# Gated delta-rule attention and softplus MLP on one core: head pairs over two batches, single inverses for chunks 0 and 1, a new order of work

## The chip, the core and the metric

The kernel runs on one core of a Trainium2 chip. TensorE (PE; its weight loads are listed apart as PEld) multiplies matrices into PSUM, VectorE (DVE), ScalarE (ACT) and GpSimd (POOL) do the rest, and SyncE (SP), ACT and POOL issue the transfers. Each engine takes its own instructions in their order and waits on semaphores for the others. The metric is device time in microseconds (us), the median of several runs; lower is better.

## What is computed

Each of 32 sequences (4 batches x 8 heads) of 768 tokens with 48 features keeps a 48x48 state. The output of all heads goes, token by token, through a two-layer MLP.

```python
k_n = k / (norm(k) + 1e-6)
for t in range(768):                        # per batch b and head h
    y[t]  = g[t] * (q[t] @ state)
    v_old = k_n[t] @ state
    state = state + beta[t] * outer(k_n[t], v[t] - v_old)
x   = y as [3072 tokens, 384]               # 8 heads x 48
out = softplus(x @ w_in) @ w_out            # 384 -> 2048 -> 384
```

## The kernel before

**Tiling.** The 768 tokens are 12 chunks of 64. In a chunk the recurrence becomes matrix products: the gram matrix of the keys, the inverse of a triangular 64x64 matrix for each sequence, and products with the state. The 32 sequences lie as 2 partition halves (`r`, batches 2r and 2r+1) times 16 units. Small matmuls have 64 rows by 64 columns of the array, so four tiles: row half by column half.

**Stages of a chunk.** `norms` (L341): squares, a row reduction (`red`), root, `eps`. `front` (L388): `cast` or `kmul` scales and casts k and q, `trs` transposes them on PE, `kev`/`qev` evict to `kqt`, `gram` (L516) multiplies, `kkc` and `mask` (L498) evict. `inverse` (L567) works for a group of chunks: `ln` transposes 32x32 blocks so that each lane has its own small matrix, `prep` scales it, 15 `step`s of a multiply (L664) and an add (L671) invert the 16x16 diagonal blocks on DVE or POOL, `ca`, `cb` and three `st` transposes (L714) bring them back, and `xmm`, `tmm`, `zmm` on PE join the blocks. `chain` (L811) is the recurrence from chunk to chunk: `ks` and `qs` (L826) multiply keys and queries with the state, `w`, `umm` (L880), `zu` (L893), `smm` (L910) with the state's update `s`, `ymm` (L936) for the output product, `y` (times g), `ytr` (transposes) and `xt`. `dense` (L976) is the MLP: `g1` (L989) into bank `h`, `soft` (L1001, softplus on ACT), `g2` (L1016) into bank `o`, `o` (eviction), `store`. Jobs are one chunk for chunks 0, 1, 10 and 11, and two chunks between.

**Groups.** `GROUPS` joins two chunks to one inverse, so that the lanes hold both; chunks 0 and 1 are group 0. For that group (`DIAGONALS`) `gramd` (L540) multiplies the 32x32 diagonal blocks apart, 64 matmuls a chunk, so that `ln` needs them alone. Chunks 0 and 1 are `RAW`: their keys are used without norm, and `lbeta` (L580 to L583) puts the norms into beta.

**Pairs.** Two heads of one batch (`2i`, `2i+1`, the index `m`) share a transposed tile; `p` is the batch in a half. The loops that use the units in turn walk

```python
CROSS = [(r, p, i, m) for i in range(NP) for m in range(2) for p in range(2) for r in range(2)]
```

`umm` and `zu` read half `r` and write half `r ^ p`. `ymm` reads rows `HALF[r]` and writes columns `HALF[r]`, bank `yp[m]`.

**Order.** Nothing is scheduled while it runs. Every piece of work is an item with a number, and `_ORDER` (L1066) lists them in one sequence, each with its engine's letter (P, D, A, G for POOL, S for SP). An engine's queue is its items in this sequence; buffers are handed out and returned in it too. `fill` items (L1046) are four matmuls of the identity into bank `h` whose result isn't used; 40 exist, 13 stand in the order, two of them behind the first `g1`. Loads are issued by SP: two of 192 KB for each of k, q, v and g a chunk, in 192-byte rows but for q (1,536 bytes). The weights are issued by POOL, w_in and w_out in four parts each, between its other work.

Of the kernel before, what the change touches and what calls it, by code (L numbers as in the profile page):

```python
# [11 lines left out]
F16 = mybir.dt.float16  # L12
# [68 lines left out]
GROUPS = [[0, 1], [2, 3], [4, 5], [6, 7], [8, 9], [10, 11]]  # L81
GROUP_OF = [i for i, cs in enumerate(GROUPS) for _ in cs]
INV_ENG = ["DG"] * 6
N_FILL = 40
DIAGONALS = (0,)

@with_exitstack
def kernel(
# [11 lines left out]
    nc = tc.nc  # L100
# [39 lines left out]
    r_kn = ring("kn", 4, [P, 2, H, 64], F16)  # L140
# [35 lines left out]
    make_identity(nc, ident32)  # L176
    for r in range(2):
        for x in range(2):
            l0 = 32 * (2 * r + x)
            bt = beta[2 * r : 2 * r + 2].rearrange("p h (c l) -> c (p h) l", l=C)  # L180
            nc.gpsimd.dma_start(
                out=beta_l[l0 : l0 + 32, 0], in_=bt[:2, :, HC * x : HC * x + HC]
            )
# [23 lines left out]
    def copy(en, o, x, sign=1):  # L207
# [9 lines left out]
        [(r_kk, 0, 1), (r_td, 0, 1), (r_z, 1, 0), (r_z, 1, 1)],  # L217
        [(r_, n, a) for r_ in (r_kk, r_td) for n in (1, 2) for a in range(2)]
# [23 lines left out]
    for n in range(1, 4):  # L242
# [7 lines left out]
        for i in FIXED[n] if n < 3 else []:  # L250
# [3 lines left out]
            if i[0] is r_z or i[2] == 0 or n == 1:  # L254
                i[0].init.setdefault(i[1], []).append(setup[n][-1])
    beta_it = []
    for r in range(2):
        for x in range(2):
            for a in range(2):

                def bload(en, r=r, x=x, a=a):
# [3 lines left out]
                        out=beta_l[l0 : l0 + 16, 1:],  # L265
# [12 lines left out]
    def heads(ap, m):  # L278
        return ap.rearrange("p a (i m) d -> p (a i) m d", m=2)[:, :, m]
# [11 lines left out]
    def load(name, x, r, c, b2):  # L291
# [5 lines left out]
        def fn(en):  # L297
            if name == "q":
                src = x[:, b2::2, t0 : t0 + C].rearrange(
                    "b i (g j) d -> b i g (j d)", j=8  # L300
                )
                ENG[en].dma_start(out=b.ap[:, b2].rearrange("p h d -> p (h d)"), in_=src)
                return
            o = b.ap[64 * b2 : 64 * b2 + 64]
# [5 lines left out]
        its.append(add("load", f"{name}{c}.{b2}", "S", fn, bufs=[b], size=192))  # L310

    for c in range(NC):
        for name, x, r in (("k", k, r_f), ("q", q, r_f), ("v", v, r_f), ("g", g, r_f)):
            for b2 in range(2):
                load(name, x, r, c, b2)
# [19 lines left out]
    kd_of, kd_it = {}, {}  # L335
# [5 lines left out]
    def norms(c):  # L341
        kf, kl = tiles["k", c]
        ksq = Buf(r_f)
        if RAW[c] and c % 2:
            nv = nv_of[c - 1]
        else:
            nv = Buf(r_nv)
# [7 lines left out]
        n0 = NU * (c % 2) if RAW[c] else 0  # L355

        def nvs():
            return nv.ap[:, n0 : n0 + NU]
# [804 lines left out]
```

## Time and profile before

| | |
|---|---|
| runs | 242.04, 242.27, 242.74 us, median 242.27 |
| profiled execution | span 241.5 us from first to last instruction (its own time isn't listed; the runs' median is 0.77 above the span) |
| dense matmuls on PE | L1016 77.7 us, L989 74.0 us |
| fills (L1046) on PE | 18.1 us |
| softplus (L1001) on ACT | 56.5 us |
| DMA | 27.57 MB, 114 GB/s mean |
| chain that ended last | PE 75%, DMA 7%, DVE 6%, SP's queue 4%, issue 3%, ACT 2%, POOL 1% |

The page's slices (40 of 6 us, tenths of busy time, the last lines the granted TensorE clock and the DMA engines):

```
PE   7645877879988999999999999999999999999983
DVE  2768699888897889987899757896496310623000
ACT  5767576764982778876895767757363674143540
POOL 8740393875779778989597482016620000000000
PEclk9985599999999999999999999999999999999999
DMA  6999989999999399961889514962302311303112
```

In a group of the profile, "x384 | 8.5, 187 | 0.4 <-DVE u" means 384 instructions, 8.5 us of busy time together (overlaps count once), 187 ns for one, and 0.4 us in which the engine was idle just before them, with what ended the wait. A line can be that of a helper: L209, L211 and L213 are `copy`, told apart by their tiles. "SPq" is SP's queue of transfers.

### The profile page before, as it was taken

To read this page: it belongs to the slowest core of one execution; us is meant where nothing else is said; L and a number is where in the kernel's file an instruction comes from. 1 tells how busy PE (TensorE), PEld (TensorE's weight loads), DVE (VectorE), ACT (ScalarE), POOL (GpSimd) and SP (SyncE) were. 2 spreads that over 40 slices of the span, in tenths; PEclk is the share of its full clock that TensorE was granted. 3 is DMA by queue.
4 is the path that set the end of the run, shared out by engine and by line. 5 is a ranking of instruction groups with operands and counts; after the bars stand their busy time and mean duration, and the time that the engine had idled before them with its cause. 6 is when DMAs were issued, how large, how long until landed. Compare 5 with 4: busy or idle time off the path is not lost.

```text
span 241.5 us, 11396 instructions
## 1 busy us (share of the span) xinstructions
PE 219.4 (91%) x5020; PEld 135.6 (56%) x5020; DVE 161.7 (67%) x368; ACT 152.8 (63%) x292; POOL 113.7 (47%) x197
## 2 busy tenths in 40 slices
PE   7645877879988999999999999999999999999983
PEld 2423455646764664556655566655565555677751
DVE  2768699888897889987899757896496310623000
ACT  5767576764982778876895767757363674143540
POOL 8740393875779778989597482016620000000000
PEclk9985599999999999999999999999999999999999
DMA  6999989999999399961889514962302311303112
GB/s 102 182 245 137 167 135 190 176 173 180 180 217 167 57 177 164 162 113 35 150 153 184 97 30 94 160 122 52 69 21 52 68 34 25 64 19 81 35 33 65
DMA packets 86833, 27.57 MB, mean 114 GB/s; under 512 B 77048, under 2 KB 86776, under 8 KB 86784
## 3 DMA queue, kind: packets, MB, share of 16 engines
q1 hardware_dynamic: 80624, 20.83, 52.6%
q0 software_dynamic: 3840, 3.17, 8.5%
q10 hardware_dynamic: 2320, 2.85, 5.2%
q8 instruction: 39, 0.64, 1.2%
q14 instruction: 10, 0.08, 0.1%
HBM read 25.26 MB, written 4.72 MB: 124 GB/s over the span
## 4 chain that ended last, share of the span: by engine, by line
PE 75%; DMA 7%; DVE 6%; SPq 4%; issue 3%; ACT 2%; POOL 1%; DVEq 0%; ACTq 0%; POOLq 0%
PE o L1016 27%; PE h L989 26%; DMA w_in<-in_moe_w_in_dram 4%; PE d L826 3%; SPq L305 3%; PE d L936 3%; PE d L516 2%; DMA f<-in_q_dram 2%; PE d L422 2%; PE d L963 2%; PE d L454 2%; PE d L880 2%; PE d L910 2%; PE d L893 2%; PE d L768 1%
## 5 line engine op out<-in xcount | busy, mean ns | idle before, releaser
L1016 PE MATMUL o<-w_out,ga 128*128 128x384 f16 x384 | 77.7, 327 | 0.7 <-ACT osb L209 0.6
L1001 ACT ACTIVATE ga<-h 128x512 f16<-128x512 f32 x96 | 56.5, 599 | 29.8 <-PE h L989 25.9
L989 PE MATMUL h<-xt,w_in 128*128 128x512 f16 (+1 forms) x384 | 74.0, 327 | 0.5 <-DMA w_in<-in_moe_w_in_dram 0.3
L989 PEld LDWEIGHTS <-w_in 128*128 128x128 f16 x384 | 34.5, 98 | 21.2 <-DMA w_in<-in_moe_w_in_dram 0.8
L1016 PEld LDWEIGHTS <-ga 128*128 128x128 f16 x384 | 33.7, 98 | 21.8 <-issue 0.8
L664 POOL TENSOR_TENSOR tmp<-nn,tt 128x78 f32<-128x78 f32 (+7 forms) x53 | 19.2, 362 | 16.1 <-DVE tt L671 13.0
L373 POOL TENSOR_TENSOR nv<-nv,half_c 128x16 f32<-128x16 f32 x8 | 23.5, 2940 | 6.6 <-DVE nv L362 6.5
L671 POOL TENSOR_TENSOR tt<-tt,tmp 128x78 f32<-128x78 f32 (+7 forms) x53 | 20.4, 385 | 4.2
L498 DVE TENSOR_TENSOR mt<-d,mask 128x256 f16<-128x256 f32 x48 | 18.2, 413 | 4.5 <-PE d L516 3.5
L209 ACT ACTIVATE kqt<-d 128x1024 f16<-128x1024 f16 (+1 forms) x18 | 18.0, 1000 | 4.8 <-PE d L454 3.6
L211 DVE CAST u<-d 128x384 f16<-128x384 f32 x20 | 10.9, 554 | 14.3 <-PE d L880 7.9
L209 ACT ACTIVATE u<-d 128x384 f16<-128x384 f32 x28 | 13.0, 490 | 11.8 <-PE d L880 5.4
L1046 PE MATMUL h<-ident 128*128 128x512 f16 x52 | 18.1, 493 | 1.7 <-DVE ident L197 1.7
L209 ACT ACTIVATE kk<-d 128x256 f16<-128x256 f32 x37 | 13.4, 386 | 6.3 <-PE d L516 5.4
L209 ACT ACTIVATE osb<-o 128x384 f32<-128x384 f32 x19 | 9.3, 492 | 9.4 <-PE o L1016 9.3
L454 PE MATMUL d<-ident,qn 128*128 128x128 f16 x96 | 8.5, 243 | 6.7 <-ACT qn L209 5.9
L950 DVE TENSOR_TENSOR yg<-d,f 128x384 f16<-128x384 f32 x24 | 12.3, 551 | 2.9 <-PE d L936 2.8
L924 DVE TENSOR_TENSOR s<-s,d 128x384 f16<-128x384 f16 x20 | 10.4, 542 | 5.7 <-PE d L910 4.3
L644 POOL TENSOR_TENSOR nn<-ln,beta_l 128x256 f32<-128x256 f16 x8 | 6.1, 780 | 14.2 <-DVE ln L627 14.2
L209 ACT ACTIVATE xt<-d 128x768 f16<-128x768 f16 x10 | 8.1, 813 | 7.0 <-PE d L963 7.0
L866 DVE TENSOR_TENSOR w<-f,d 128x384 f16<-128x384 f32 x22 | 11.3, 545 | 1.4 <-ACT xt L209 0.7
L362 DVE TENSOR_REDUCE nv<-f 128x16 f32<-128x768 f32 x12 | 11.3, 942 | 1.0 <-ACT f L351 1.0
(117 smaller groups left out, 346.7 us busy)
## 6 DMA issues: line engine op xcount, KB each, us to landing
f<-in_k_dram SPq DMA_DIRECT2D x24, 192.0 KB, 5.7
f<-in_q_dram SPq DMA_DIRECT2D x24, 192.0 KB, 5.6
f<-in_v_dram SPq DMA_DIRECT2D x24, 192.0 KB, 5.3
f<-in_g_dram SPq DMA_DIRECT2D x24, 192.0 KB, 5.3
out_dram<-osb ACTq DMA_DIRECT2D x29, 96.0 KB, 2.7
out_dram<-osb SPq DMA_DIRECT2D x19, 96.0 KB, 2.8
w_in<-in_moe_w_in_dram POOLq DMA_DIRECT2D x4, 384.0 KB, 7.9
w_out<-in_moe_w_out_dram POOLq DMA_DIRECT2D x4, 384.0 KB, 8.4
```

The costliest lines, as they stand in the source:

```text
L209: nc.scalar.activation(o, x, AF.Copy, scale=float(sign))
L362: lambda en: nc.vector.tensor_reduce(nvs().rearrange("p (a h) -> p a h", a=2), ksq.ap, mybir.AxisListType.X, ALU.add),
L373: nc.gpsimd.tensor_tensor(nvs(), nvs(), half_c[:, :NU], ALU.pow)
L454: nc.tensor.transpose(o[:, j], qn.ap[:, j].rearrange("p m d -> p (m d)"), ident)
L498: nc.vector.tensor_tensor(mt[c][m].ap[:, NP * p : NP * p + NP], gb[m].ap.rearrange("p (i b) -> p i b", i=NP)[:, :, n : n + C], mask[:, Non ...
L664: ENG[en].tensor_tensor(t, nn.ap[:, :, j : j + 1, j + 1 :].broadcast_to([P, 2, w, n]), tt.ap[:, :, :w, j : j + 1].broadcast_to([P, 2, w, n ...
L671: ENG[en].tensor_tensor(rows, rows, t, ALU.add)
L950: lambda en, m=m: nc.vector.tensor_tensor(heads(yg.ap, m), hd(yp[m].ap), heads(gf.ap, m), ALU.mult),
L989: nc.tensor.matmul(hp.ap[:, n * b : n * b + n], w_in[:, j, f * P : (f + 1) * P], xt.ap[:, j, t0 : t0 + n], start=(j == 0), stop=(j == 2),)
L1001: lambda en, hp=hp, o=gb: nc.scalar.activation(o.ap, hp.ap, AF.Softplus),
L1016: nc.tensor.matmul(op.ap[:, :DM], b.ap[:, col + c0 : col + c0 + 128], w_out[:, f, :], start=(f == 0), stop=(f == NF - 1),)
L1046: nc.tensor.matmul(hp.ap, ident, ident[:, None, :].broadcast_to([P, 4, P]))
```

## The change

- **Pairs over two batches.** The unit that shares a transposed tile is now one head in the two batches of a half: `m` is the batch, `h` the head. `CROSS` becomes `(r, m, h)`, with `r` fastest. `kn` is laid out `[P, H, 2, 64]`. Every product uses half `r ^ m` where it used `r ^ p`; `qs` and `ymm` write columns `HALF[r ^ m]`, so the rows of `y` for `m = 1` hold the other half's batch. So g is loaded in the matching order, and the stores name the other rows. `smm` takes 48 columns of `kn` where it took 64. The sequence of tiles in `umm`, `zu` and `zmm` stays the same four.
- **Loads.** q and g come in four loads of 96 KB a chunk, one for each half and batch, in place of two of 192 KB; rows are as long as before. SP issues 96 loads before and 144 after. The first beta loads bring chunks 0 and 1 into two slots.
- **Own inverses.** `GROUPS` starts with `[0], [1]`; there are seven groups. `gramd`, `kd` and their buffers are gone: `ln` reads the gram evictions. Chunks 0 and 1 each have their own norms, `lbeta`, `ln`, `prep`, 15 steps and transposes (half as large, and without the lane masks of a pair).
- **Last group in another bank.** The last `g2` of chunk 11 writes a bank of ring `d` instead of `o`.
- **New order.** `_ORDER` is replaced. 13 fills stand in it, all ahead of the first `g1`. Among what moves: on SP the four loads of q0 are complete with the 20th issue (13th before, with two loads); on ACT the `cast` of q0 stands ahead of chunk 1's `sqrt`; on DVE chunk 1's `eps`, `lbeta` and `ln` stand ahead of chunk 0's last step; on POOL the first w_in part stands behind chunk 1's steps 0, 1, 2, 4 and 5 (step 3 is DVE's, behind chunk 0's masks, `st`, `xs` and `w0`), and the first w_out part behind chunk 4's `kmul`; on PE the first `g2` stands right behind chunk 1's `ymm`; the two last products of chunk 11 alternate, and of the last four stores one is on SP and three on ACT, among these both of the last product.

```diff
-GROUPS = [[0, 1], [2, 3], [4, 5], [6, 7], [8, 9], [10, 11]]
+GROUPS = [[0], [1], [2, 3], [4, 5], [6, 7], [8, 9], [10, 11]]
-INV_ENG = ["DG"] * 6
+INV_ENG = ["DG"] * 7
-DIAGONALS = (0,)
-    r_kn = ring("kn", 4, [P, 2, H, 64], F16)
+    r_kn = ring("kn", 4, [P, H, 2, 64], F16)
-    CROSS = [
-        (r, p, i, m)
-        for i in range(NP)
-        for m in range(2)
-        for p in range(2)
-        for r in range(2)
-    ]
+    CROSS = [(r, m, h) for h in range(H) for m in range(2) for r in range(2)]
+    BATCH = [(r, m) for r in range(2) for m in range(2)]
...
+            if name in "qg":
+                r, m = b2
+                dst = b.ap[HALF[r], m]
+                if name == "q":
+                    src = x[2 * r + m, :, t0 : t0 + C].rearrange("h (g j) d -> h g (j d)", j=8)
+                    ENG[en].dma_start(out=dst.rearrange("p h d -> p (h d)"), in_=src)
+                else:
+                    src = x[2 * (r ^ m) + m, :, t0 : t0 + C]
+                    ENG[en].dma_start(out=dst, in_=src.rearrange("h t d -> t h d"))
...
-        def with_state(off, o, start):
+        def with_state(off, o, start, cross=0):
...
-                            hd(o[m].ap)[HALF[r], pi],
+                            hd(o[m].ap)[HALF[r ^ (cross & m)], pi],
...
         def ymm(en):
-            for r, p, i, m in CROSS:
+            for r, m, h in CROSS:
                 nc.tensor.matmul(
-                    hd(yp[m].ap)[HALF[r], NP * p + i],
-                    mt[c][m].ap[HALF[r], NP * p + i],
-                    u2[r ^ p].ap[HALF[r], 2 * i + m],
+                    hd(yp[m].ap)[HALF[r ^ m], h],
+                    mt[c][m].ap[HALF[r], h],
+                    u2[r ^ m].ap[HALF[r], h],
...
-                op = Buf(p_o)
+                op = Buf(p_d if c == NC - 1 and p else p_o)
...
-                        r0 = (2 * hf + p) * S + c * C
+                        r0 = (2 * (hf ^ p) + p) * S + c * C
```

More of the change, by code (lines that the diff above doesn't have):

```diff
@@ L308, in fn @@
             )
-        its.append(add("load", f"{name}{c}.{b2}", "S", fn, bufs=[b], size=192))
+        its.append(add("load", f"{name}{c}.{n}", "S", fn, bufs=[b],
+                       size=96 if name in "qg" else 192))
     for c in range(NC):
         for name, x, r in (("k", k, r_f), ("q", q, r_f), ("v", v, r_f), ("g", g, r_f)):
-            for b2 in range(2):
-                load(name, x, r, c, b2)
+            for n, b2 in enumerate(BATCH if name in "qg" else range(2)):
+                load(name, x, r, c, b2, n)
     wl = [[], []]
@@ L343, in norms @@
         ksq = Buf(r_f)
[L344 to L347, printed above, removed]
+        nv = Buf(r_nv)
         def square(en):
@@ L612, in lnt @@
                 )
-        l1 = add("ln", tag, "D", lnt, deps=kd_it[gi] if compact else kdeps,
-                 bufs=[kd_of[gi] if compact else kk, ln], size=nw * HC)
-        if pair and not compact:
+        l1 = add("ln", tag, "D", lnt, deps=kdeps,
+                 bufs=[kk, ln], size=nw * HC)
+        if pair:
             def pick(en):
```

302 lines of the change are left out of this document (132 added, 170 removed).

## The prediction, before the result was known

> **What bounds the kernel now.** First the page: the span, the busy shares and the slices.
>
> ```profile
> span 241.5 us, 11396 instructions
> ...
> PE 219.4 (91%) x5020; PEld 135.6 (56%) x5020; DVE 161.7 (67%) x368; ACT 152.8 (63%) x292; POOL 113.7 (47%) x197
> ```
>
> TensorE is busy for 91% of the span, no other engine above 67%. Next the table of windows tells where the missing 9% are.
>
> ```profile
> 20.00:30.00 10.00, 7.97 (x67) 3.67 (x69) 7.56 (x22) 6.77 (x10) 1.82 (x2) 0.50 1.06 145
> 30.00:40.00 10.00, 7.63 (x310) 5.04 (x302) 9.39 (x21) 7.49 (x17) 7.81 (x12) 0.98 0.97 155
> 40.00:60.00 20.00, 17.12 (x450) 12.49 (x450) 17.49 (x41) 11.40 (x26) 13.27 (x19) 1.00 1.15 178
> 60.00:80.00 20.00, 17.99 (x502) 12.80 (x500) 17.51 (x35) 14.26 (x30) 16.23 (x18) 1.00 1.14 187
> 80.00:100.00 20.00, 19.91 (x482) 11.81 (x481) 17.87 (x38) 15.90 (x28) 16.17 (x34) 1.00 0.79 129
> 200.00:220.00 20.00, 20.00 (x432) 13.56 (x431) 7.76 (x15) 7.35 (x15) 0.00 (x0) 1.00 0.20 42
> ```
>
> Columns: length, busy time of PE, PEld, VectorE (DVE), ScalarE (ACT), GpSimd (POOL), granted clock, share of the DMA engines, GB/s. From 80 us on TensorE has no gap, so time comes off there only with TensorE work. From 40 to 80 us it idles 40 - 17.12 - 17.99 = 4.89 us; VectorE is at 9.39 of 10 and 17.5 of 20, and the DMA share is about 1 or above. Before 40 us TensorE waits for chunk 0 and runs fill matmuls. The chain of waits shows how the dense work begins:
>
> ```profile
> 31.69 8.77 DMA w_in<-in_moe_w_in_dram
> 40.51 1.49 PE h L989 x12
> ...
> 58.84 0.86 PE h L1046 x4
> ```
>
> The first dense matmul waits for w_in, issued on POOL's queue; one fill (L1046) stands inside the chain at 58.84. So the end is: start of dense work (40.5) + TensorE work after it + gaps + a tail. I price the four.
>
> **Output product.** Before, ymm (L936) reads rows r and writes columns r, so only two of the four 64x64 tiles are used. zu (L893) and umm (L880) have the same 64x48 matmuls, 32 per chunk, over four tiles. TensorE's timeline late in the kernel, where nothing is waited for (start, length of the group of 32):
>
> ```profile
> 206.49 0.69 PE L936 MATMUL d<-u,mt 64*64 64x48 f16 x32
> ...
> 210.22 0.44 PE L880 MATMUL d<-w,td 64*64 64x48 f16 x32
> 213.31 0.44 PE L893 MATMUL d<-u,z 64*64 64x48 f16 x32
> ```
>
> After the change ymm walks rows r and columns r^m as those do: 0.69 - 0.44 = 0.25 us less a chunk. Over all chunks the groups say the same: 8.5 us for 384 against 5.4 us, 0.26 a chunk.
>
> ```profile
> L936 PE MATMUL d<-u,mt 64*64 64x48 f16 x384 | 8.5, 187 | 0.4 <-DVE u L211 0.3
> L880 PE MATMUL d<-w,td 64*64 64x48 f16 x384 | 5.4, 188 | 2.1 <-ACT kqt L209 0.9 <-DVE td L211 0.5 <-DVE w L866 0.5
> ```
>
> Chunk 0's ymm lies ahead of the dense start, beside the wait for w_in; eleven are on the path: **-2.75 us** (bounds -2.9 and 0). The other products keep four tiles, only in another order: nothing.
>
> The Trainium skill ("TensorE: Matmul & The Clock Gate", Part 1) speaks against this: starts of matmuls never come closer than about 25 ns, however small they are. By it 32 matmuls could not take less than 31 x 25 = 775 ns and the pairing would gain 0 instead of 2.75. The trace disagrees: one matmul is 188 ns (group of L880), so 0.44 us means starts (440 - 188)/31 = 8 ns apart, and for L936 (690 - 187)/31 = 16 ns.
>
> **Fills.** The order has 13 fills before and after, but two of the 13 stood behind the dense start; now all 13 stand ahead of it. The one in the chain goes: **-0.9** (between -0.9 and 0, if another wait fills its place). The other was beside a wait already: nothing. The 128 small matmuls of the diagonal blocks (L540) also go; they run ahead of the dense start, while the path there goes through loads: nothing.
>
> **Own inverses for chunks 0 and 1.** They run on VectorE and POOL. VectorE's durations, and POOL's for the same step:
>
> ```profile
> L671 POOL TENSOR_TENSOR tt<-tt,tmp 128x78 f32<-128x78 f32 (+7 forms) x53 | 20.4, 385 | 4.2
> L671 DVE TENSOR_TENSOR tt<-tt,tmp 128x120 f32<-128x120 f32 (+7 forms) x31 | 8.1, 261 | 1.1
> L664 DVE TENSOR_TENSOR tmp<-nn,tt 128x120 f32<-128x120 f32 (+7 forms) x31 | 8.0, 257 | 2.4 <-POOL tt L671 1.8
> L597 DVE STREAM_TRANSPOSE ln<-dn 128x512 uint32<-128x512 uint32 x1 | 1.0, 1047 | 0.9 <-ACT dn L209 0.9
> L644 DVE TENSOR_TENSOR nn<-ln,beta_l 128x256 f32<-128x256 f16 x2 | 0.9, 426 | 0.1
> ```
>
> A step is one L664 and one L671, 0.52 us on VectorE. Before, VectorE runs 14 steps of group 0, and five steps of the next group ahead of chunk 1's output: 19. After, it runs 8 of chunk 0 and 4 of chunk 1 and none of the next group ahead of that point: 12, so 3.6 us less. Against that stand one ln more (1.05), two preps of the next group that POOL did (0.85), and another lbeta, about 1.0 as an estimate (four small instructions, L580 to L583, that stand between 11.93 and 12.98 in the timeline below). The st transposes halve and double. Net 3.6 - 2.9 = 0.7 us less in a queue that is over 87% busy in this stretch: **-0.7** for the stretch behind 40 us. POOL gets some 17 more steps, which it does in the idle time ahead of 30 us (busy 1.82 of 10 from 20 to 30). Bounds: -5 (every gap between 40 and 80 us goes) to +4 (as below, were it all late).
>
> **Start of dense work.** Timeline and, for the loads, the durations of SP's issues up to 36 us (min/median/max in ns):
>
> ```profile
> 11.93 0.21 DVE L580 STREAM_TRANSPOSE nl<-nv 128x32 f32<-128x32 f32 x1
> 12.79 0.19 DVE L583 TENSOR_TENSOR bl<-bl,nl 128x32 f32<-128x32 f32 x1
> 18.36 0.84 ACT L209 ACTIVATE qn<-f 128x768 f16<-128x768 f32 x1 [0.21 <-DMA f<-in_q_dram]
> 24.34 0.21 DVE L671 TENSOR_TENSOR tt<-tt,tmp 128x30 f32<-128x30 f32 x1
> 30.87 1.62 POOL L330 DMA_DIRECT2D w_in<-in_moe_w_in_dram  x2
> ```
>
> ```profile
> L305 SPq DMA_DIRECT2D f<-in_k_dram x12: 601/734/2407, 0.8 to 31.9; - x12
> L302 SPq DMA_DIRECT2D f<-in_q_dram x10: 597/598/1777, 4.3 to 16.0; - x10
> ```
>
> Before, chunk 0's last step ends at 24.34 + 0.21 = 24.55. After, its first step no longer waits for chunk 1, but ahead of its last step VectorE's queue holds eps, lbeta and ln of chunk 1; eps waits for ScalarE's sqrt of chunk 1, and that stands behind the cast of q0, which now needs four loads. The fourth is the 20th issue on SP (before, q0's last was the 13th). The bytes ahead are about the same, and the cast began at 18.36 then; I take the same. Behind the cast: cast 0.84, sqrt, eps and diag at 0.2 each (as L580 and L583), lbeta 1.0, ln 1.05, the last step 0.5: 4.0, so 22.4, some 2 us earlier. But the first w_in issue now stands behind five of chunk 1's steps on POOL; step 3 is on VectorE, behind what chunk 0 still needs: four masks (0.41 each), three half transposes (0.54 each) and eight others (a reduction, copies, xs, w0, the step itself) that I take at 0.45 as an estimate between these two rows:
>
> ```profile
> L498 DVE TENSOR_TENSOR mt<-d,mask 128x256 f16<-128x256 f32 x48 | 18.2, 413 | 4.5 <-PE d L516 3.5 <-ACT kk L209 0.7
> L714 DVE STREAM_TRANSPOSE td<-tw 128x512 uint32<-128x512 uint32 x6 | 6.5, 1086 | 0.0
> ```
>
> 1.65 + 1.63 + 3.6 = 6.9 us. So w_in's issue comes at 22.4 + 6.9 + two POOL steps (two instructions of 0.385 each, so 1.5) = 30.8, where the issue that was waited for began at 31.69. That is too near to call: **0**, bounds -2 and +6.
>
> **Weights.** w_out's first part moves from before the chunk-4 kmul on POOL to behind it.
>
> ```profile
> 36.06 1.56 POOL L330 DMA_DIRECT2D w_out<-in_moe_w_out_dram  x2
> 46.07 1.47 POOL L406 TENSOR_TENSOR kn<-f,nv 128x768 f16<-128x768 f32 x1 [0.73 <-DVE nv L383]
> 56.06 0.98 PE L936 MATMUL d<-u,mt 64*64 64x48 f16 x32
> w_out<-in_moe_w_out_dram POOLq DMA_DIRECT2D x4, 384.0 KB, 8.4
> ```
>
> If kmul stays at 46.07, the issue starts at 47.5 and lands at 55.9. The first second-layer product now stands right behind chunk 1's ymm, which was at 56.06 and would be some 1.6 earlier: a wait of about 1.0 after ymm's own time. **+1.0**, bounds 0 and +4. TensorE takes its queue in order, so all dense work waits with it.
>
> **SP's queue.** q and g come in four loads a chunk instead of two: 48 issues more, at 0.6 us some 29 us of SP. SP was held up by its queue in this stretch (DMA share above 1), so I take 0; if that cover is gone, it is the rival below.
>
> **Tail.** The last product goes to another bank, so it does not wait for the eviction of the one before:
>
> ```profile
> 234.25 0.49 ACT L209 ACTIVATE osb<-o 128x384 f32<-128x384 f32 x1 [0.92 <-PE o L1016]
> ...
> 234.79 2.76 PE L1016 MATMUL o<-w_out,ga 128*128 128x384 f16 x16 [0.58 <-ACT osb L209]
> ...
> 237.59 0.49 ACT L209 ACTIVATE osb<-o 128x384 f32<-128x384 f32 x1 [2.85 <-PE o L1016]
> 238.10 0.47 SPq L1035 DMA_DIRECT2D out_dram<-osb  x1
> 238.11 0.50 ACTq L1035 DMA_DIRECT2D out_dram<-osb  x1
> ```
>
> The gap of 0.58 goes. But the last two stores, one on SP and one on ScalarE before, now both stand on ScalarE's queue: +0.50. Net **-0.1**.
>
> **Sum.** -2.75 - 0.9 - 0.7 + 0 + 1.0 - 0.1 = -3.45. The span of 241.5 becomes 238.05. The profiled execution's own time is not listed; the median of the runs, 242.27, lies 0.77 above the span, and I add that: **238.8 us**.
>
> **Rivals.**
> 1. The start runs smoother still: of the 4.89 us of gaps between 40 and 80 us another 2 to 4 go, because chunk 1's chain no longer shares its inverse with chunk 0. Time 235 to 237. For it: VectorE's queue is the fuller one there. Against it: the DMA share above 1 in both windows. Chance 0.12.
> 2. The change doesn't do what it says: ymm stays at 0.69 us, because the two banks that it writes or the rate of issue hold it, not the tiles. 238.8 + 2.75 = 241.6. The 0.44 us of L880, which writes two banks too, speaks against it. Together with a saving that gaps elsewhere swallow: 0.13. (The Trainium skill's page on TensorE, quoted above, would give this case.)
> 3. Slower: SP's issues become the bound at the start. Place: the 20th issue, q0's last part. At 0.73 us an issue it is out at 0.8 + 20 x 0.73 = 15.4; at 1.0 us (the maxima of 1.8 and 2.4 show that it can be) at 20.8. With 5.6 us to landing (row below) the cast starts at 21.0 or at 26.4, against my 18.36. All of chunk 0 hangs on it, and the w_in issue too, one for one. It decides from 18.36 + 3.45 + 0.8 = 22.6 on; with 0.93 us an issue, 25 us, the time is 238.8 + 6.6 = 245. For it: the order puts 13 q loads into the first 24 issues. Against it: the DMA share of 1.06. Chance 0.18.
> 4. w_out arrives late by the full bound and w_in's later parts with it: 238.8 + 5 = 243.8. Chance 0.12.
>
> ```profile
> f<-in_q_dram SPq DMA_DIRECT2D x24, 192.0 KB, 5.6
> ```
>
> **Numbers.** The forecast, 237 to 240.8, has 0.45. A difference under 0.3% (0.7 us) can't be told from none here. Faster: 0.45 + 0.12 + 0.05 of rival 2 = 0.62. Same: 0.08 of rival 2 + 0.02 of rival 4 = 0.10. Slower: 0.18 + 0.10 = 0.28. The range runs from 235.5 (leaving out the lower part of rival 1) to 244.6 (leaving out the upper half of rival 3); about 0.13 is left out.
>
> **What the changed profile would show.** ymm's group at about 5.4 to 5.8 us for 384, 0.44 us a chunk; else the first term is wrong. TensorE idle between 40 and 80 us at 4 to 6 us, with no wait of h or o on w_in or w_out above 1.5 us; else the weights were mis-sized. ScalarE's cast of q0 before 20 us; if after 22.6, rival 3. The first dense matmul at 39 to 42 us. The last sixteen L1016 without the 0.58 wait on osb. The whole is wrong if the stretch behind 80 us is no longer free of gaps: I moved nothing there, and the new order moves everything.

## The result and the profile after

The changed kernel takes 254.9 us (median of four runs: 252.6, 252.9, 256.9, 258.2), the kernel before 242.5 beside it: ratio **1.040, 95% interval 1.031 to 1.048**. The ratio leaves out runs more than 1.5% above the fastest of their kernel, here the two upper ones and one of the kernel before (246.4 us). The kernel is slower by some 10 us, where 3.5 us less were forecast. The profiled execution took 252.9 us with a span of 251.2. First its page (span; busy time, share and instructions; the shares of the chain that ended last):

```profile
span 251.2 us, 11245 instructions
...
PE 221.2 (88%) x4892; PEld 134.9 (54%) x4892; DVE 168.4 (67%) x384; ACT 152.7 (61%) x298; POOL 115.5 (46%) x215
...
PE 67%; DVE 10%; DMA 7%; SPq 6%; issue 5%; ACT 3%; POOL 1%; ACTq 0%; DVEq 0%; POOLq 0%
```

TensorE idles 30.0 us instead of 22.1, and is busy 1.8 us more. The windows of the kernel after, with the same columns and stretches as those of before, tell where:

```profile
20.00:30.00 10.00, 7.89 (x106) 4.40 (x106) 7.63 (x20) 7.72 (x13) 6.35 (x15) 0.83 0.89 167
30.00:40.00 10.00, 7.80 (x269) 5.10 (x269) 8.91 (x24) 7.24 (x15) 6.86 (x15) 1.00 1.06 166
40.00:60.00 20.00, 16.17 (x392) 11.79 (x383) 14.46 (x34) 15.78 (x31) 14.89 (x27) 0.74 1.19 182
60.00:80.00 20.00, 17.33 (x489) 12.55 (x487) 15.80 (x34) 13.66 (x26) 13.27 (x19) 1.00 0.90 153
80.00:100.00 20.00, 19.66 (x487) 11.97 (x486) 16.60 (x40) 14.44 (x29) 10.98 (x18) 1.00 0.85 166
100.00:120.00 20.00, 16.99 (x391) 8.85 (x393) 16.38 (x34) 12.20 (x25) 10.99 (x14) 0.91 0.51 90
200.00:220.00 20.00, 20.00 (x442) 11.23 (x440) 7.89 (x16) 10.72 (x22) 0.00 (x0) 1.00 0.10 22
```

From 40 to 80 us 6.5 us are idle (4.9 before), at a clock of 0.74 in the first half (1.00 before). And the stretch behind 80 us, free of gaps before, now has holes: 3.0 us from 100 to 120 alone.

A ruler for the rest. Each chunk's output product is one group of 32 matmuls in TensorE's timeline (start, length), so its ends cut the kernel into stretches. With the order of before these hold the same work; the new order spreads the dense work otherwise, so there TensorE's busy and idle time have to be read apart. The fourth, fifth and last, first of the kernel before (the fourth's first 27), then of the one after:

```profile
86.58 0.59 PE L936 MATMUL d<-u,mt 64*64 64x48 f16 x27
109.47 0.67 PE L936 MATMUL d<-u,mt 64*64 64x48 f16 x32
218.35 0.69 PE L936 MATMUL d<-u,mt 64*64 64x48 f16 x32
```

```profile
88.82 0.62 PE L893 MATMUL d<-u,mt 64*64 64x48 f16 x32
117.43 0.44 PE L893 MATMUL d<-u,mt 64*64 64x48 f16 x32
225.43 0.44 PE L893 MATMUL d<-u,mt 64*64 64x48 f16 x32
```

The ends of the output products (us), read in the same way in the profiled runs of the experiments below:

| kernel | 1st | 4th | 5th | last | span |
|---|---|---|---|---|---|
| before | 37.7 | 87.3 | 110.1 | 219.0 | 241.5 |
| after | 36.8 | 89.4 | 117.9 | 225.9 | 251.2 |
| before, q and g in four loads (b2) | 41.0 | 92.0 | 114.7 | 223.4 | 245.8 |
| pairs alone (p1) | 40.3 | 92.8 | 115.4 | 223.5 | 245.9 |
| pairs alone, k2 early (p7) | 42.9 | 93.1 | 116.3 | 226.4 | 248.8 |
| after, two loads (a6) | 34.5 | 85.7 | 113.7 | 224.0 | 249.2 |
| after, o first (a7) | 38.1 | 90.9 | 118.0 | 227.0 | 252.3 |
| after, ln 4 early (a9) | 38.1 | 94.2 | 122.6 | 232.0 | 257.3 |

After against before: +2.1 us up to the fourth, **+5.7 from the fourth to the fifth** (28.5 against 22.8), -0.9 to the last, +2.8 behind it; sum 9.7, the difference of the spans. The windows between these ends part TensorE's busy and idle time (us):

| stretch | before: busy, idle | after: busy, idle |
|---|---|---|
| up to the fourth | 69.9, 17.4 | 70.6, 18.9 |
| fourth to fifth | 22.8, 0.1 | 25.3, 3.1 |
| fifth to last | 108.8, 0.1 | 104.6, 3.4 |
| behind the last | 17.9, 4.6 | 20.8, 4.5 |

The 2.8 us of the tail are work, not waiting: the new order leaves three g1 items and two g2 items more for it, and these are missing between the fifth and the last. So the -0.9 there hides 3.3 us of new gaps, about as many as the stretch before it has. Idle time grows by 7.9 us in all, busy time by 1.8. "Pairs alone" is different: it loses all its time ahead of the fourth.

### The profile page after: what moved, and what is told of

Its sections match the earlier page's. It is cut to its first block, busy times and chain, and to the rows that moved or that the text cites. A ratio compares the mean times of both kernels' runs of the same rounds, so it can differ in the third digit from the quotient of the medians.

```text
span 251.2 us, 11245 instructions
## 1 busy us (share of the span) xinstructions
PE 221.2 (88%) x4892; PEld 134.9 (54%) x4892; DVE 168.4 (67%) x384; ACT 152.7 (61%) x298; POOL 115.5 (46%) x215
## 4 chain that ended last, share of the span: by engine, by line
PE 67%; DVE 10%; DMA 7%; SPq 6%; issue 5%; ACT 3%; POOL 1%; ACTq 0%; DVEq 0%; POOLq 0%
PE o L973 23%; PE h L946 22%; DMA w_out<-in_moe_w_out_dram 3%; SPq L295 3%; PE d L788 3%; DVE mt L495 2%; PE d L513 2%; SPq L301 2%; PE d L453 2%; DMA f<-in_q_dram 2%; PE d L853 2%; PE d L421 2%; PE d L920 2%; DMA f<-in_k_dram 1%; PE d L893 1%
## 5 line engine op out<-in xcount | busy, mean ns | idle before, releaser
L973 PE MATMUL o<-w_out,ga 128*128 128x384 f16 x368 | 75.8, 329 | 4.0 <-ACT osb L209 2.4
L946 PE MATMUL h<-xt,w_in 128*128 128x512 f16 (+1 forms) x384 | 76.6, 338 | 1.6 <-ACT ga L958 1.3
L946 PEld LDWEIGHTS <-w_in 128*128 128x128 f16 x384 | 36.6, 101 | 24.9 <-issue 4.0
L627 POOL TENSOR_TENSOR tmp<-nn,tt 128x78 f32<-128x78 f32 (+7 forms) x68 | 24.6, 362 | 28.7 <-DVE tt L634 21.3
L634 POOL TENSOR_TENSOR tt<-tt,tmp 128x78 f32<-128x78 f32 (+7 forms) x68 | 25.2, 371 | 5.3
L209 ACT ACTIVATE u<-d 128x384 f16<-128x384 f32 x29 | 13.8, 491 | 10.2 <-PE d L853 7.7
L1003 PE MATMUL h<-ident 128*128 128x512 f16 x52 | 17.2, 477 | 1.7 <-DVE ident L197 1.7
L513 PE MATMUL d<-kqt 48*64 48x128 f16 (+1 forms) x448 | 11.2, 225 | 2.0 <-DVE s L211 0.8
L421 PE MATMUL d<-ident,kn 128*128 128x128 f16 x96 | 8.4, 235 | 5.1 <-DVE kn L211 1.9
L513 PEld LDWEIGHTS <-kqt 48*64 48x64 f16 x448 | 7.9, 114 | 8.5 <-issue 5.6
```

The source lines that it names most:

```text
L209: nc.scalar.activation(o, x, AF.Copy, scale=float(sign))
L421: nc.tensor.transpose(o[:, NP * p + i], kn[c].ap[:, NP * p + i].rearrange("p m d -> p (m d)"), ident,)
L513: nc.tensor.matmul(gb[m].ap.rearrange("p (i b) -> p i b", i=NP)[HALF[r], i, lo:hi], x[:, :C], x[:, lo:hi],)
L627: ENG[en].tensor_tensor(t, nn.ap[:, :, j : j + 1, j + 1 :].broadcast_to([P, 2, w, n]), tt.ap[:, :, :w, j : j + 1].broadcast_to([P, 2, w, n ...
L634: ENG[en].tensor_tensor(rows, rows, t, ALU.add)
L946: nc.tensor.matmul(hp.ap[:, n * b : n * b + n], w_in[:, j, f * P : (f + 1) * P], xt.ap[:, j, t0 : t0 + n], start=(j == 0), stop=(j == 2),)
```

## The experiments

The theory at the start: the gaps behind the dense start come from a halved clock or from queues that stand behind one copy. The rival: SP's queue of issues. All ratios are to the kernel before, run on the same chip, with 95% intervals.

**Pairs alone.** The kernel before with the new pairs and q and g in four loads, everything else (groups, order, fills) as before.

```diff
-    for b2 in range(2): load(name, x, r, c, b2)
+    for n, b2 in enumerate(BATCH if name in "qg" else range(2)): load(name, x, r, c, b2, n)
     # and the new heads, CROSS, ymm, stores; _ORDER of before, each q and g item twice
```

> The kernel before with the new head pairs alone: groups, diagonal products, fills, tail bank and order stay as before; only each load of q and g becomes two issues in the same place of SP's queue. Theory (the new order is what costs, the pairs are worth what ymm saves): ymm 5.5 us for 384 instead of 8.5, the time 2 to 3 us under the kernel before, about 239.7. Rival (the pairs cost something themselves, by 48 more issues on SP or by the changed layouts): not faster, 242.5 to 248, with q loads landing late or evictions longer than before.

Ratio 1.0243 [1.0169, 1.0318], although the output product falls as forecast. One part that was to gain costs 6 us.

**No fills behind the dense start; three fills more.** Two runs on the clock: the kernel before without its two late fills (removed lines), and the kernel after with three more, ahead of gram 2.0, ks 1 and the transposes of k3 (added lines).

```diff
-P150
-P164
...
+P177 P351
+P178 P799
+P183 P366
```

> The kernel before without the two fills that stand behind the start of the dense work; nothing else changes. Theory (the fills hold TensorE's clock up in the gaps of 40 to 60 us): the granted clock falls to about 0.5 for some us between 45 and 60 us, and the time rises by 1 to 5 us, to 243.5 to 247.5. Rival (the prediction's own term): the clock stays at 1.0 and the time falls by up to 0.9 us, to 241.6.

> The changed kernel with three fills (of four matmuls) put into TensorE's queue where it idles between 38 and 44 us: ahead of the second gram of chunk 2, ahead of ks of chunk 1, and ahead of chunk 3's transposes. Theory (the gap halves the clock from about 43 to 53 us, which costs some 4 us of dense work): clock 1.0 from 42 to 54 us and 3 to 5 us off the changed kernel's 252.8, about 248.5. Rival (TensorE waits for VectorE's queue in that stretch at either clock): clock 1.0, but less than 1 us off.

Without the fills 0.998 [0.992, 1.005]: no difference. With three more 1.062 [1.053, 1.071], slower than after: the clock in the window of 40 to 60 us rose from 0.74 to 0.98, and fell to 0.85 in the next. Filling the gaps to raise the clock gained nothing; this run does not part the clock from the time of the fills themselves.

**Copies ahead of masks.** On the kernel after, 15 copies of the gram (kkc) that stood behind a mask which reads the same bank go ahead of it (c, p, m as in the order's tags).

```diff
-mask c.pm ... kkc c.pm
+kkc c.pm mask c.pm
```

> The changed kernel with one change of order: for the 15 pairs of evictions of one bank in which VectorE's mask stands ahead of ScalarE's kkc, kkc now stands ahead. Theory (ScalarE waits 9.4 us for masks, with softplus and the evictions of the second layer queued behind it, and that opens the gaps behind 80 us and the second fall of the clock at 105 us): that wait under 2 us, the gap at 100 to 104 us gone, 3 to 6 us off 252.8, about 248.5. Rival (VectorE's own queue is late there, and PE waits for its masks and transposes either way): less than 1 us off, with the gap moved.

1.047 [1.039, 1.055], no gain. The wait for osb at 100 us fell from 2.4 to 0.3 us, and larger waits stand between 60 and 80 us (TensorE 14.69 of 20; 2.6 us for w_out, 2.4 for an inverse's transpose).

**Four loads, and nothing else.** The kernel before with q and g, and with q alone, in four issues.

```diff
-                src = x[:, b2::2, t0 : t0 + C].rearrange("b i (g j) d -> b i g (j d)", j=8)
-                ENG[en].dma_start(out=b.ap[:, b2]..., in_=src)
+                b2, r = divmod(n, 2)
+                src = x[2 * r : 2 * r + 2, b2::2, t0 : t0 + C].rearrange(...)
+                ENG[en].dma_start(out=b.ap[HALF[r], b2]..., in_=src)
```

> The kernel before, with q and g of each chunk loaded in four issues of 96 KB instead of two of 192 KB, at the same places of the order; heads, tiles, engines and all else as before. Theory, SP's issues: six of the ten issues added for q0 to q4 stand ahead of q0's last part, at some 0.6 us each, so q0 lands 3 to 4 us later, SP stays behind for some 25 us, and the kernel takes 5 to 9 us more, a ratio of 1.02 to 1.04 to the kernel before; SP's share of the chain goes up from 4% to 8 or 9%, the DMA share of 10 to 20 us falls from 1.20 to some 0.75. Rival, the pairing itself (other strides, other copies): nothing here, ratio 1.00, the DMA share as before.

> The same with q alone in four issues and g in two as before. Theory, SP's issues at the start: nearly all of the loss of the kernel with both, since q0 to q4 stand in the first 18 places of SP and g0 behind them: ratio 1.02 to 1.035. If SP is the bound all the way and not at the start alone: about half of the loss with both. Rival, the pairing itself: 1.00.

Ratios 1.0242 [1.011, 1.037] and 1.0233 [1.012, 1.035]: **splitting the loads alone costs what "pairs alone" costs**, and q's are enough. SP's timeline (start, length, count), first before, then q in four:

```profile
4.32 1.59 SPq L302 DMA_DIRECT2D f<-in_q_dram  x2
...
9.78 6.83 SPq L302 DMA_DIRECT2D f<-in_q_dram  x8
```

```profile
4.61 2.78 SPq L303 DMA_DIRECT2D f<-in_q_dram  x4
...
11.48 10.71 SPq L303 DMA_DIRECT2D f<-in_q_dram  x16
```

The eight issues of 192 KB took 0.85 us each on average, 230 GB/s, the sixteen of 96 KB 0.67 us each, 147 GB/s. The shortest took about 0.6 us in both (597 ns in the row of L302 that the prediction shows; 0.60 in the chain of waits with q in four), whatever their bytes. So with q in four SP issues back to back at its shortest, and what stands behind these loads in its queue goes out later. The windows of 15 to 20 us, before and q in four, show the DMA engines half used (share 1.10 to 0.50, 249 to 174 GB/s):

```profile
15.00:20.00 5.00, 1.06 (x23) 0.95 (x23) 3.64 (x15) 3.56 (x8) 0.66 (x2) 0.68 1.10 249
```

```profile
15.00:20.00 5.00, 2.77 (x68) 1.20 (x64) 2.55 (x8) 4.25 (x10) 1.94 (x5) 0.83 0.50 174
```

**A second queue.** Half of the early q loads issued by ScalarE, in the pairs alone (q0 to q4, shown) and in the kernel after (q0 to q3).

```diff
-S53 S51 S41 S39 S29 S27 S77 S75 S65 S63
+A53 A51 A41 A39 A29 A27 A77 A75 A65 A63
```

> The pairs alone, with two of the four issues of q0 to q4 given by ScalarE's queue instead of SP's, in the same places of the order, so that SP has as many issues up to there as before. Theory, SP's issues: q0's cast comes back to about 18 us, the DMA share of 10 to 20 us goes back above 1, and of the 8.6 us by which pairs alone missed the 239.8 that the output product alone would give, most comes back: ratio 0.985 to 1.005, below the kernel before if g's issues cost nothing. Rival, the pairing itself: still 1.02. A third way, in which ScalarE stands waiting at its own issues: 1.01 to 1.02 with ScalarE's casts late.

> The kernel after, with two of the four issues of q0 to q3 given by ScalarE's queue. Theory, SP's issues at the start: q0's cast from 20.7 back to some 18 us, the dense work starts 1.5 to 2 us earlier, and with later loads early as well 2 to 5 us less: ratio 1.02 to 1.03. Rival, the new order and the own inverses are what costs: still 1.04.

1.0266 [1.016, 1.038] and 1.039 [1.027, 1.051]: nothing came back. As built, every load of SP and ScalarE from the ninth on waits until the load eight places before it has landed. With q in four on SP alone that wait never showed; with two queues the view of waits of the pairs' run has it on SP (in total, times, longest):

```profile
SPq L295 <- DMA f<-in_k_dram: 1.3, 1, 1.3
SPq L298 <- DMA f<-in_q_dram: 1.2, 1, 1.2
SPq L301 <- DMA f<-in_k_dram: 1.1, 1, 1.1
```

The flow hardly rises, though two engines issue (15 to 20 us of this run):

```profile
15.00:20.00 5.00, 1.51 (x36) 0.68 (x34) 3.25 (x10) 2.25 (x5) 2.08 (x5) 1.00 0.56 180
```

The trace has a second limit for it: a q load of 192 KB is signalled as landed sixteen times, one of 96 KB eight times (and once at its issue), and the share stays near half of the sixteen DMA engines with one queue (0.50) and with two (0.56). This fits small q loads that all run on the same eight engines; no run changes that alone. And ScalarE now stands at its own issues (idle 2.84 us ahead of 20.09), so that q0's cast comes at 21.88 us, later than the 19.75 of the pairs alone. So the run does not test SP's issues by themselves. The Trainium skill ("DMA: Bandwidth & Descriptors", "Issuing engines are not separate DMA queues") says that issuing from several engines saves only the time that the sequencer needs to start a transfer. In this run saving that time on SP gained nothing (1.0266 against 1.0243).

**The loads of before, in both kernels.** Pairs alone, and the kernel after, with q and g in two loads of 192 KB. The right rows are left out, so only the time is read.

```diff
-            if name in "qg":
-                r, m = b2
-                ...
+            if name == "q":
+                src = x[:, b2::2, t0 : t0 + C].rearrange("b i (g j) d -> b i g (j d)", j=8)
+                ...
```

> The pairs alone, but q and g of each chunk loaded as the kernel before loads them, in two issues of 192 KB at the same places of the order. It leaves the right places of q's heads and g's batches out: the bytes and the issues are those of before, the rows that they bring are others, so the output is not the reference's and only the time is read. Theory, the loss is in the count of issues and nothing in the pairing itself: the start is as before (the fourth output product ends near 87.3 us, not 92.8) and the output products save 1 to 2.75 us: ratio 0.987 to 0.997. Rival, the pairing costs as much elsewhere as the output product saves: 0.998 to 1.003. If the loads were not the cause: 1.02.

> The kernel after with the same two loads of 192 KB for q and for g (again rows from other heads and batches, so that only the time is read), each issued at the place of the later of the two that it stands for; own inverses, engines and all other places as in after. Theory A, the issues alone: what splitting q and g costs, 5 to 6 us, comes back, ratio 1.01 to 1.02, and the gaps of TensorE at 100 to 104 us go. Theory B, the new order and the own inverses have a loss of their own in the stretch behind 89 us: that stretch (fourth to last output product) keeps its 136 us against 131.7, and the ratio stays at 1.025 to 1.04.

Pairs alone: **1.0047 [1.0006, 1.0088]**. Against 1.0243 the loads cost 2.0% of 243 us, 4.8 us. And the pairs with the loads of before are no gain: the 2.75 us do not reach the time. After: **1.0398 [1.035, 1.045]**, no better than after with four loads, though its fourth output product is 3.7 us earlier (85.7). It needs 28.0 us from there to the fifth, much as after does, and TensorE then idles 5.7 us up to the last where it idled 3.4. So with equal loads the new order and the own inverses cost 1.040 - 1.005, some 8.5 us.

**Which load is the late one?** Two runs on the order of SP's queue in the pairs alone: q2 behind q0 and q1, and chunk 2's keys (k2) ahead of q4 and q3. SP's queue, one entry a load; q2 later, then k2 early:

```diff
-q2 q2 q2 q2
 v0 v0 k3 q1 q1 q1 q1 q0 q0 q0 q0
+q2 q2 q2 q2
 q4 q4 q4 q4 q3 q3 q3 q3
```

```diff
 q0 q0 q0 q0
+k2 k2
 q4 q4 q4 q4 q3 q3 q3 q3 k3 beta g0 g0 beta
-k2
 beta
-k2
```

> The pairs alone with all four issues a chunk, and q2's four issues, its cast, its transposes and its eviction moved behind those of q0 and q1 (q2 stood ahead of v0 and k3). Theory, SP's issues at some 0.64 us each: q0 lands 4 x 0.64 = 2.6 us earlier and of the 4.5 us by which the fourth output product is late some 2 come back: ratio 1.012 to 1.02. Rival, the time at which all of the first 40 issues are through is what counts, whatever their order: no change, 1.024.

> The pairs alone with all four issues a chunk, and one thing moved in SP's queue: the two loads of chunk 2's keys (k2), which stood behind the eight issues of q4 and q3, both of k3 and two of g0, go ahead of q4 and q3, right behind q0. With the pairs alone GpSimd waits 12.0 us for k2 and squares it at 31.17 us, before at 26.91: 4.3 us later, as much as the fourth output product is late (92.8 against 87.3, less what came before). Moving q2 behind q0 brought q0's cast back to 16 us and gained nothing, so it is not q0. Theory, the loss is k2's late landing, set by the number of SP's issues ahead of it at 0.60 to 0.65 us each: with some 10 issues fewer ahead k2 lands 5 to 6 us earlier and most of the 4.8 us that the four issues cost come back: ratio 1.004 to 1.012, the fourth output product at 88 to 90 us. Rival, every load behind has to be through, whatever the order: no change, 1.02 to 1.025.

q2 later: 1.0232 [1.019, 1.028], nothing gained, although q0's cast on ScalarE (the second cast of a q) came from 19.75 us, in the pairs alone, to 16.66:

```profile
19.75 0.84 ACT L209 ACTIVATE qn<-f 128x768 f16<-128x768 f32 x1 [0.66 <-DMA f<-in_q_dram]
```

```profile
16.66 0.85 ACT L209 ACTIVATE qn<-f 128x768 f16<-128x768 f32 x1
```

k2 early: 1.0332 [1.028, 1.039], no better than the pairs alone. GpSimd's timeline, pairs alone, then with k2 early:

```profile
31.17 1.47 POOL L350 TENSOR_TENSOR f<-f 128x768 f32<-128x768 f32 x1 [12.04 <-DMA f<-in_k_dram]
32.97 0.60 POOL L211 COPY tx<-tb 64x512 f16<-64x512 f16 x1 [0.33 <-DVE tb L712]
```

```profile
22.39 1.47 POOL L350 TENSOR_TENSOR f<-f 128x768 f32<-128x768 f32 x1 [3.00 <-DMA f<-in_k_dram]
35.11 0.61 POOL L211 COPY tx<-tb 64x512 f16<-64x512 f16 x1 [11.26 <-DVE tb L712]
```

k2 is there almost 9 us earlier, and the next instruction, the copy `tx` of chunk 0's inverse, stands 2 us later. So neither q0 nor k2 carries the cost. The first run met its rival (no change); k2 early came out above both of its ranges.

The traces name another load: the second of k3. ScalarE squares chunk 3's keys ahead of the cast of q4 and of the copies that chunk 0's inverse needs, and it waits for that load. Before, pairs alone, k2 early:

```profile
23.25 0.84 ACT L351 ACTIVATE f<-f 128x768 f32<-128x768 f32 x1 [0.43 <-DMA f<-in_k_dram]
```

```profile
26.58 0.84 ACT L348 ACTIVATE f<-f 128x768 f32<-128x768 f32 x1 [2.37 <-DMA f<-in_k_dram]
```

```profile
28.73 0.84 ACT L348 ACTIVATE f<-f 128x768 f32<-128x768 f32 x1 [4.32 <-DMA f<-in_k_dram]
```

| kernel | place of k3's second load on SP | square of k3 (us) | `tx` on GpSimd | first w_in issue |
|---|---|---|---|---|
| before | 18 | 23.25 | 29.64 | 30.87 |
| q and g in four (b2) | 28 | 26.95 | 33.34 | 34.56 |
| q in four (b3) | 28 | 28.19 | 34.59 | 35.81 |
| pairs alone (p1) | 28 | 26.58 | 32.97 | 34.19 |
| q2 later (p5) | 28 | 26.71 | 33.04 | 34.26 |
| k2 early (p7) | 30 | 28.73 | 35.11 | 36.34 |

`tx` follows the square by 6.3 to 6.4 us in every row, and the first issue of w_in by another 1.2. The first move left ten issues more ahead of k3's load than before has, the second made it twelve. No run moved that load ahead, so this is read from the traces and not tested.

**The gap at 100 us.** In the kernel after TensorE's largest gap (its timeline, then ScalarE's) is a chain of queues: TensorE waits for the copy of `osb` (o 1.1), which on ScalarE stands behind a copy `kk` that waits 2.89 us for VectorE's mask.

```profile
103.30 0.81 PE L973 MATMUL o<-w_out,ga 128*128 128x384 f16 x4 [2.37 <-ACT osb L209]
104.76 2.66 PE L946 MATMUL h<-xt,w_in 128*128 128x512 f16 x6 [0.65 <-ACT ga L958]
```

```profile
102.49 0.38 ACT L209 ACTIVATE kk<-d 128x256 f16<-128x256 f32 x1 [2.89 <-DVE mt L495]
102.77 0.48 ACT L209 ACTIVATE osb<-o 128x384 f32<-128x384 f32 x1
```

In the order (549 and 554 are the copies kkc 7.01 and 7.11, 1051 is o 1.1, 1093 a second-layer product, 1067 and 1063 are softplus):

```diff
-A549 A1051 P1093 A554 A1067 A1063
+A1051 P1093 A1067 A1063 A549 A554
```

> The kernel after with two copies on ScalarE (kkc 7.01 and 7.11) moved three instructions back, behind the copy of the second matmul's result (o 1.1) and two softplus; nothing else. In after these copies stood waiting 2.9 us for VectorE's masks at 102.5 us, and TensorE behind them 2.4 us for the bank that o 1.1 frees. Theory, an in-order queue: the wait of 2.4 us goes, the dense work runs on while VectorE catches up, the clock does not fall at 104 to 108 us, and of the 5.7 us by which the stretch from the fourth to the fifth output product is longer than before (28.5 against 22.8) 2 to 4 come back: ratio 1.025 to 1.033. Rival, VectorE's chain of steps is late anyway and TensorE stands a little later for it: no change, 1.04.

And with it the first two loads of w_out ahead of chunk 4's kmul on GpSimd:

```diff
+wload w1.0 wload w1.1
 kmul 4.0
-wload w1.1 wload w1.0
```

> The same as the one with o 1.1 first, and the first two loads of w_out issued ahead of chunk 4's kmul on GpSimd. Theory: the wait of 1.1 us for w_out at 59 us goes: 1 us less than the one with o 1.1 first. Rival: the work behind it stands 1 us later for the recurrence, no change.

1.0402 [1.034, 1.046]: no change, the rival held. The 2.4 us at osb went, and TensorE now waits for `dn`, a transpose of the inverse of chunks 4 and 5:

```profile
106.26 0.43 PE L707 MATMUL d<-dn,kk 64*64 64x32 f16 x32 [1.31 <-DVE dn L677]
107.39 1.73 PE L946 MATMUL h<-xt,w_in 128*128 128x512 f16 x6 [0.71 <-ACT ga L958]
```

The run with w_out early as well scattered from 248.0 to 256.6 us (median 254.1) and decides nothing.

**The places of the inverses.** VectorE's timeline of the joint inverses: the transpose `ln` that starts chunks 4 and 5, `dn` that ends it, `ln` of chunks 6 and 7. Before, then after:

```profile
78.05 1.96 DVE L604 STREAM_TRANSPOSE ln<-kk 128x1024 uint32<-128x1024 uint32 x1
...
96.97 1.08 DVE L714 STREAM_TRANSPOSE dn<-ta 128x512 uint32<-128x512 uint32 x1
99.03 1.92 DVE L604 STREAM_TRANSPOSE ln<-kk 128x1024 uint32<-128x1024 uint32 x1
```

```profile
85.50 1.92 DVE L567 STREAM_TRANSPOSE ln<-kk 128x1024 uint32<-128x1024 uint32 x1
...
103.72 1.06 DVE L677 STREAM_TRANSPOSE dn<-ta 128x512 uint32<-128x512 uint32 x1
...
110.61 1.93 DVE L567 STREAM_TRANSPOSE ln<-kk 128x1024 uint32<-128x1024 uint32 x1
```

From `ln` to `dn` the inverse of chunks 4 and 5 takes 18.9 us before and 18.2 after, but the first starts 7.5 us later and the second 11.6. So the next theory was that the order starts the inverses too late. VectorE's items there (463 mask 5.01, 837 and 836 w 3, 834 xt 2, 469 to 475 ln 4 to step 4.0):

```diff
-D463 D837 D836 D834 D469 D470 D473 D474 D475
+D469 D470 D473 D474 D475 D463 D837 D836 D834
```

> The kernel after with the start of the joint inverse of chunks 4 and 5 (ln 4, pick, two preps, the first step) moved ahead of one mask, chunk 3's two w and one xt on VectorE, as it stands in before. In after that inverse starts at 85.50 us, 18.9 us behind the end of the one before it, in before at 78.05, 14.0 us behind. Theory, the chain of inverses sets the stretch from the fourth to the fifth output product: the inverse starts 1.5 to 2.4 us earlier, the fifth output product comes as much earlier, TensorE's idle time falls by 1 to 2 us, and so does the time: ratio 1.032 to 1.036. Rival, chunk 3's own recurrence, held up by 3 us of VectorE's work ahead of it, loses as much: 1.04.

The second run moves ln 6 as well, and on ScalarE the four copies that it reads; the third has the loads of before with both:

```diff
-st 4.c xs 4.0 xs 4.1 st 4.b ln 6 pick 6
+st 4.c ln 6 pick 6 xs 4.0 xs 4.1 st 4.b
```

> The same, and the start of the inverse of chunks 6 and 7 with it: the four copies that it needs go in one row on ScalarE behind chunk 4's two casts, and ln 6 and pick 6 right behind the transposes of the inverse of chunks 4 and 5, as in before, where it starts 2.1 us behind that inverse's first transpose; in after it starts 6.9 us behind, at 110.6. Theory: this inverse starts 3 to 5 us earlier, and the time falls by 3 to 5 us in all: ratio 1.02 to 1.028. Rival as above: 1.04; or the second move alone counts: 1.03.

> The same as the last, with q and g loaded in two issues of 192 KB as before does (rows of other heads and batches: the right rows are left out, only the time is read). Theory: with the inverses early the start is no longer given back at 86 to 114 us, so what the loads cost in after comes out: 2 us less than the kernel without that, ratio 1.01 to 1.02, near the 1.0047 of the pairs alone with these loads. Rival, a loss in the new order that is neither: still 1.03 or more.

1.062 [1.057, 1.067], 1.068 [1.063, 1.073] and 1.061 [1.055, 1.067]: the theory fell. With ln 4 ahead, it is chunk 3's own products that come late, and VectorE then stands 6.1 us at their output, with the rest of the inverse queued behind (waits of VectorE, 84 to 110 us):

```profile
DVE yg L907 <- PE d L893: 6.1, 1, 6.1
```

**Tail bank alone.** The kernel before with the last tile's sums in a bank of ring `d`.

```diff
-                op = Buf(p_o)
+                op = Buf(p_d if c == NC - 1 and p else p_o)
```

> The kernel before with the bank of the last group of the second product alone: the last output tile's sums go to a bank of the other pool, as in after. Theory: the one wait of TensorE behind 90 us, 0.58 us for the copy of osb, goes and nothing takes its place: 0.3 to 0.6 us less, ratio 0.9975 to 0.999. Rival: the store that ends last stands where it stood, 1.000.

0.9989 [0.995, 1.003]: the wait of 0.58 us is gone from the trace, and the time can't be told from no change. No variant with the pairs came below the kernel before.

## Why the prediction was wrong, point by point

Two steps failed: SP's queue, which was put at 0, and the new order, which had no term at all and holds the end of the kernel after.

**Step "SP's queue": failed.** The prediction priced 48 more issues at 29 us of SP and then took 0, because "SP was held up by its queue in this stretch (DMA share above 1)". That cover was the size of the loads: with q in 96 KB the share fell to 0.50, SP issued back to back, and k3's load behind them went out later. Measured with the order of before: 4.8 us. In the kernel after, taking the split back gains nothing (1.0398 against 1.040), so there this cost is hidden behind the next. Rival 3 named the mechanism but hung it on q0 alone (and its 245 leaves out the 0.8 us of slack that it grants: 244.6). In the kernel after q0's cast is late, by 2.35 us, short of the bound of 22.6 that the rival set:

```profile
20.71 0.84 ACT L209 ACTIVATE qn<-f 128x768 f16<-128x768 f32 x1 [2.49 <-DMA f<-in_q_dram]
```

but in the pairs alone q0 is not what the cost hangs on: early or late, the time was the same.

**"The new order moves everything": failed where the prediction had priced nothing.** It named a stretch behind 80 us with gaps as the case in which the whole is wrong, gave it no term and no chance, and that is what came: from the fourth output product to the last TensorE idles 6.6 us where it idled 0.2. With the loads of before it idles 8.9 us there and the time is no better, so in the kernel after it is this that holds the end, and the loads are only a cost ahead of it. Which instruction holds it stays open: four runs went at single places (clock, copies behind masks, osb, ln), and none made it faster. The own inverses were not tried without the order; their 15 steps more (2 on VectorE, 13 on GpSimd) may be part of that loss, and the runs don't part them. The sign of 4 to 6 us of idle time from 40 to 80 us was missed too, with 6.5.

**Output product: right in size, wrong as a gain.** The three products of 64x48, columns as in the groups quoted before:

```profile
L853 PE MATMUL d<-u,z 64*64 64x48 f16 x384 | 5.9, 189 | 1.5 <-issue 1.3 <-ACT u L209 0.2
L893 PE MATMUL d<-u,mt 64*64 64x48 f16 x384 | 5.6, 189 | 1.1 <-issue 1.1
L840 PE MATMUL d<-w,td 64*64 64x48 f16 x384 | 5.5, 188 | 0.3 <-ACT td L209 0.3
```

8.5 became 5.6 us, -2.9 against -2.75 forecast, and 0.44 us a group of 32 is starts 8 ns apart. But with the loads of before the pairs gave +0.5% and not -1.1%. From the fourth to the last output product, where TensorE has hardly a gap, the pairs alone take 130.7 us against 131.4 of the same loads without pairs. The groups of that stretch, first without pairs (b2), then with them:

```profile
L944 PE MATMUL d<-u,mt 64*64 64x48 f16 x256 | 5.4, 187 | 0.0
```

```profile
L928 PE MATMUL d<-u,mt 64*64 64x48 f16 x256 | 3.6, 189 | 0.0
```

Of the 1.8 us saved there 0.7 reach the time: TensorE's busy time falls by 1.3 us in that stretch, and its idle time grows by 0.6 (0.1 to 0.7). What the new gaps wait for was not traced.

**Start of dense work: 0 forecast, +1.65.** The first dense product began at 40.51 us; now, inside the bounds of -2 and +6, as below. The first issue of w_in came at 33.39 us where 30.8 was worked out, some 2.6 later, nearly what q0's cast is late by.

```profile
42.16 0.83 PE L946 MATMUL h<-xt,w_in 128*128 128x256 f16 x6
```

**Weights: right in size, by luck.** The wait was put at 1.0 us. It is 1.09, but both sides of it came later than taken: kmul at 49.10 us (46.07 taken), so w_out landed at 59.1 instead of 55.9, and chunk 1's output product ended at 58.0.

```profile
59.10 0.81 PE L973 MATMUL o<-w_out,ga 128*128 128x384 f16 x4 [1.09 <-DMA w_out<-in_moe_w_out_dram]
```

**Fills: failed, small.** -0.9 was taken for the fill in the chain; without both late fills the kernel before is as fast (0.998). Other waits fill the place, the upper bound that the prediction gave.

**Own inverses: not seen.** The -0.7 is inside the loss above. **Tail: right** within what can be told (-0.1 forecast; the bank alone 0.9989; idle time of the tail 4.5 us against 4.6). The work that the order left for it was not in the sum.

## What to carry to other kernels

Before a load is split, divide its bytes by the time of one issue, and look for what stands behind it in the queue: if the queue was paced by transfers only because the loads were big, the same bytes in twice the issues can be paced by issues, and a load far behind pays for all of them. Follow that load to the engine that waits for it before moving another. Price the whole new order, not only the parts that the change names: where an order is written out, the stretch that moves most is the one to bound, and closing one wait at a time may only show the next. Where an order moves work, read busy and idle time of a stretch apart, not its length. A saving on a full engine is worth its size only if nothing ahead of it costs more; try the part alone, with its side costs taken out, before believing the sum.

## What the runs showed of the hardware that was not expected

- One load issue on SP took about 0.6 us at the least for 96 KB as for 192 KB. Sixteen issues of 96 KB went back to back in 10.71 us, so SP fed 96 KB in 0.67 us, 147 GB/s; before, 192 KB in 0.85 us, 230 GB/s.
- A q load of 96 KB is signalled as landed eight times, one of 192 KB sixteen times, and the DMA share stays at 0.50 with one queue of such loads and at 0.56 with two.
- In one run a fuller clock, 0.98 instead of 0.74 from 40 to 60 us, went with a kernel 2% slower; the fills that made it are in that time.
- With the loads of before the pairs bring the output product's group from 8.5 to 5.7 us, on an engine that is busy for 90% of the span, and the time does not fall (1.0047).
